# Attention and mixture of experts in one kernel: heads handled by twos, a product moved between turned rows, and the first planned expert fetched a step sooner

## The chip, the cores and the metric

The kernel runs on one core of one Trainium2 chip. The metric is the device time of one execution in microseconds; the time before is the median of three timed runs. The profile is of one further execution.

## The reference, cut to what matters

Block-sparse attention over 4 batches, 8 heads, 768 tokens, head size 64, in blocks of 32 tokens (24 blocks): the first and last block row see all keys ("dense"), every other block row sees its three neighbours, the first and last block and three drawn blocks ("sparse"). Each of the 3072 attended tokens then goes to one of 8 experts.

```python
scores = np.where(mask, q @ k.T / sqrt(64), -1e9)
x = softmax(scores) @ v                      # tokens x 512
e = argmax(x @ w_gate)
out[t] = p_e(t) * sigmoid(x @ w_output_gate)[t, e] * (relu(x[t] @ w1[e]) @ w2[e])
```

## The kernel before, in words

**Steps.** The kernel is one long program of numbered steps. A batch pair (`bp` 0, then 1) has 26 units: 4 dense ones (`Dense(bp, u)`, u = 0 to 3, each for the head pair u and u + 4 of both batches) and 22 sparse ones (`Sparse`, two for each of 11 pairs of block rows). Step n starts unit n. So steps 0 to 3 are dense, 4 to 25 sparse, 26 to 29 dense, 30 to 51 sparse. From step 27 on the experts' work is mixed in (`mixed`, L1394); a name like `p_h(0)` there is the expert program's work item 0, and its step is 31 plus its number in `program` (`FIRST` = 31).

**A unit** runs over three steps: `pS` (scores on TensorE into two PSUM banks), `dM` (row maxima on VectorE), `aE` (exponentials on ScalarE), `pT` (turning, L490: three or four 128x128 transposes of a piece on TensorE, then a copy out of PSUM by VectorE or ScalarE), one step later `pO` (the product with V), then `fin` (division by the sum, whose first instruction, L502, is the mark `normed` that POOL's indirect DMAs of that step wait for by `behind`). A dense unit has four pieces, T0 to T3; the PSUM pool `psT` has two buffers, so T2 and T3 wait for the copies of T0 and T1.

In a dense step n the order on TensorE is `pS` of unit n, `pO` of unit n - 2, T0 and T1 of unit n - 1, T2 and T3 of unit n - 1, and on VectorE `dM` of unit n, then the copies of T0 and T1 (L1417 to 1430):

```python
if isinstance(last, Dense):
    if before: before.pO()
    now.dM()
    if isinstance(now, Dense):
        last.pT(0, "dve")
        now.aE()
        last.pT(1, "act")
```

**What sets the order.** Every engine runs its instructions in the order in which the program is written. Hooks `at(step, rank, f)` put helper work behind a stage of a step: rank 0 ahead of the maxima, 2 ahead of the turning, 3 to 5 at the end. All plain DMAs are issued from SP in that order, so an SP wait holds every later one.

**K and V on chip.** `kn[bp]` holds the keys, 128 partitions x 24 blocks x 256 values (all 8 heads of a block side by side). The start loads it in two halves of 12 blocks (1.5 MB each) and V in 6 chunks of 520 KB. `gather_k`, `window_k` and `fixed` scale blocks of 256 values into the ring `kr` for the sparse units: on POOL (L412, L434), VectorE (L441, L442) and ScalarE (L432). The keys of batch pair 1 are loaded in 12 pieces at the steps of `LOAD_K`.

**The start.** `warm(n, w)` (L172) runs `NWARM[n]` matmuls on ones: 44 of 128 columns and 21 of 512 before the first scores, 11 between the two halves of them, 8 and 8 in step 1. `setup_blocks` (L322) makes the row indices for V from the drawn blocks (`raw`); it runs whole ahead of step 0 on VectorE. `setup_rest` zeroes the row table in four DMAs.

**The first planned expert (unit 0 of `EARLY`).** Its tokens are known once 8 of the 24 token tiles are routed: `route_c` ends at step 25, four `route_d` scatters write the table (`SCATTER[1]`, L804), `choose` (L757; 13 instructions on POOL with 2 and then 4 on VectorE around them) finds the expert and `load_r` reads its number into SP's registers. `load_t` (step 27, L971) reads the table rows and waits for the scatters; `load_x` (L1010, POOL, two halves) gathers the tokens; `load_w` (L987, SP) loads the weights in pieces of 512 KB; `w_h` and `w_l` (L1068 ScalarE, L1072 VectorE) split a piece in two f16 parts from step 29 on. `x_t` (L1040, TensorE, steps 29 and 30) turns the gathered tokens, `x_l` (L1047, VectorE, steps 30 and 31) makes their low part, and `p_h(0)` (L1086, step 31) is the first product with them.

## Time and profile before

| | us |
|---|---|
| timed runs, median (lowest to highest) | 549.1 (547.7 to 552.0) |
| the profiled execution's own time | 543.43 |
| its span in the profile | 541.8 |
| TensorE busy | 510.1 (94%) |
| VectorE, ScalarE, POOL busy | 357.3, 311.5, 249.0 |

The span runs from the first to the last instruction; 1.6 us of the profiled execution lie around it. In all rows times are counted from the start of the span. "PEclk" is the granted TensorE clock as a share of full speed, "DMA share" the mean busy share of 16 DMA engines.

### The profile page before, as it was taken

To read this page: it belongs to the slowest core of one execution; us is meant where nothing else is said; L and a number is where in the kernel's file an instruction comes from. 1 tells how busy PE (TensorE), PEld (TensorE's weight loads), DVE (VectorE), ACT (ScalarE), POOL (GpSimd) and SP (SyncE) were. 2 spreads that over 40 slices of the span, in tenths; PEclk is the share of its full clock that TensorE was granted. 3 is DMA by queue.
4 is the path that set the end of the run, shared out by engine and by line. 5 is a ranking of instruction groups with operands and counts; after the bars stand their busy time and mean duration, and the time that the engine had idled before them with its cause. 6 is when DMAs were issued, how large, how long until landed. Compare 5 with 4: busy or idle time off the path is not lost. (4 is left out here: it accounts for less than half of the span.)

```text
span 541.8 us, 18874 instructions
## 1 busy us (share of the span) xinstructions
PE 510.1 (94%) x7429; PEld 358.9 (66%) x7429; DVE 357.3 (66%) x732; ACT 311.5 (57%) x584; POOL 249.0 (46%) x369
## 2 busy tenths in 40 slices
PE   8999999988879999999999999999999999999993
PEld 5466676666557667776777766677666667676671
DVE  5568577585679766876876668776755754465580
ACT  1455666665666656776666555666562663554480
POOL 3466566752755855548646337553421503211120
PEclk9999999999998999999999999999999999999997
DMA  7969988889399769887767595599998999996111
GB/s 295 280 197 306 294 259 264 237 239 298 92 327 311 202 224 301 242 230 251 220 209 227 142 343 197 203 391 402 405 301 299 325 399 313 301 326 232 28 40 37
DMA packets 60062, 137.98 MB, mean 255 GB/s; under 512 B 20471, under 2 KB 27131, under 8 KB 59708
## 3 DMA queue, kind: packets, MB, share of 16 engines
q1 hardware_dynamic: 48524, 99.93, 57.0%
q0 software_dynamic: 11296, 36.49, 21.1%
q8 instruction: 60, 0.98, 0.7%
q10 hardware_dynamic: 144, 0.26, 0.2%
q14 instruction: 38, 0.31, 0.2%
HBM read 127.88 MB, written 14.81 MB: 263 GB/s over the span
## 5 line engine op out<-in xcount | busy, mean ns | idle before, releaser
L1086 PE MATMUL h<-xb,kr 128*128 128x256 f16 (+1 forms) x780 | 86.9, 261 | 1.4 <-DMA xb<-xb 1.4
L1118 PE MATMUL S<-kr,hh 128*128 128x512 f16 x348 | 85.4, 379 | 0.0
L1086 PEld LDWEIGHTS <-kr 128*128 128x128 f16 x780 | 69.5, 98 | 19.7 <-issue 2.8
L434 POOL TENSOR_TENSOR kr<-kn,eighth 128x256 f32<-128x256 f32 x110 | 68.7, 651 | 9.1 <-issue 7.1
L534 DVE TENSOR_REDUCE mx<-S 128x4 f32<-128x1024 f32 x44 | 53.7, 1219 | 28.1 <-PE S L527 16.6
L542 ACT ACTIVATE P<-S,mx 128x256 f32<-128x256 f32 x176 | 69.1, 484 | 1.1 <-DVE mx L534 1.0
L451 POOL DMA_INDIRECT vt<-in_v_dram,vidx x44 | 45.0, 1022 | 51.5 <-DVE den L504 29.0
L1118 PEld LDWEIGHTS <-hh 128*128 128x128 f16 x384 | 36.9, 98 | 30.4
L493 ACT COPY pt<-T 128x512 f32<-128x512 f32 x66 | 36.9, 592 | 31.0 <-PE T L490 28.6
L1099 ACT ACTIVATE hh<-h 128x512 f16<-128x512 f32 (+1 forms) x36 | 19.7, 548 | 55.9 <-PE h L1086 55.4
L1010 POOL DMA_INDIRECT xb<-xscr,tab x16 | 20.7, 1295 | 63.0 <-issue 23.6
L527 PE MATMUL S<-kr,qall 64*32 64x256 f32 x1408 | 49.5, 386 | 0.0
L490 PE MATMUL T<-ident,P 128*128 128x128 f32 x352 | 46.0, 274 | 0.0
L1072 DVE SCALAR_TENSOR_TENSOR kr<-e,kr 128x1024 f16<-128x1024 f32 x32 | 38.3, 1219 | 9.8 <-ACT kr L1068 9.8
L804 POOL DMA_INDIRECT table<-vals,place x24 | 26.7, 1114 | 33.1 <-DVE den L504 21.1
L490 PEld LDWEIGHTS T<-ident,P 128*128 128x128 f32 x352 | 40.1, 143 | 1.6 <-issue 1.3
L560 PE MATMUL O<-vt,pt 128*32 128x65 f32 x1408 | 32.8, 222 | 4.7 <-issue 4.1
L1105 DVE SCALAR_TENSOR_TENSOR hh<-h,hh 128x512 f16<-128x512 f32 (+1 forms) x36 | 22.5, 626 | 19.7 <-ACT hh L1099 16.6
L1072 DVE SCALAR_TENSOR_TENSOR ws<-e,ws 128x1024 f16<-128x1024 f32 x24 | 29.9, 1246 | 7.0 <-PE h L1086 4.3
L560 PEld LDWEIGHTS O<-vt,pt 128*32 128x32 f32 x1408 | 25.6, 110 | 13.0 <-issue 8.8
L1086 PEld LDWEIGHTS <-ws 128*128 128x128 f16 x324 | 29.9, 99 | 5.4 <-issue 0.4
L1068 ACT ACTIVATE kr<-e 128x1024 f16<-128x1024 f32 x32 | 33.1, 1050 | 0.0
(349 smaller groups left out, 972.5 us busy)
## 6 DMA issues: line engine op xcount, KB each, us to landing
e<-in_wcat_dram SPq DMA_DIRECT2D x80, 512.0 KB
rk<-in_wcat_dram SPq DMA_DIRECT2D x30, 512.0 KB
vc<-in_wcat_dram SPq DMA_DIRECT2D x14, 512.0 KB
vn<-in_v_dram SPq DMA_DIRECT2D x12, 520.0 KB
xscr<-x SPq DMA_DIRECT2D x48, 128.0 KB
qall<-in_q_dram SPq DMA_DIRECT2D x23, 256.0 KB
vc<-in_v_dram SPq DMA_DIRECT2D x22, 260.0 KB
ws<-in_wcat_dram SPq DMA_DIRECT2D x8, 512.0 KB
```

Of the source, the lines that this page charges most:

```text
L434: nc.gpsimd.tensor_tensor(r[:, slot], kn[bp][:, ds(rv, 1)].rearrange("p o n -> p (o n)"), eighth.to_broadcast([128, 256]), op=ALU.mult)
L451: behind(nc.gpsimd.indirect_dma_start(vt[bp, i][:, s].rearrange("p b j w -> p (b j w)"), None, v, bass.IndirectOffsetOnAxis(ap=vidx[:, bp, ...
L490: nc.tensor.transpose(pt[:, 128 * c:128 * c + 128], p[:, 128 * c:128 * c + 128], ident)
L493: mark("copy", nc.scalar.copy(t[:, 0:w], pt[:, 0:w]))
L527: nc.tensor.matmul(s[64 * h2 + 32 * qi:64 * h2 + 32 * qi + 32, b, hp], t[p, 64 * j + 32 * qi:64 * j + 32 * qi + 32], g[p, 1 - qi:3:1 + qi, ...
L534: mark("max", nc.vector.tensor_reduce(mx, self.s.rearrange("p b h n -> p (b h) n"), axis=AX.X, op=ALU.max, negate=True))
L542: nc.scalar.activation(p[:, 256 * hp:256 * hp + 256], self.s[:, b, hp], AF.Exp, bias=self.mx[:, 2 * b + hp:2 * b + hp + 1])
L560: nc.tensor.matmul(o[row:row + 32, b, hp, 0:VW], self.t[b][:, col:col + 32], av[:, qi, b, 4 * h2 + 2 * hg + hp], start=b == 0 and hp == 0, ...
L1068: nc.scalar.activation(w[:, 0], piece(n), AF.Copy, scale=SW)
L1072: nc.vector.scalar_tensor_tensor(w[:, 1], piece(n), SW, w[:, 0], op0=ALU.mult, op1=ALU.subtract)
L1086: nc.tensor.matmul(hps[n // 2][:, cols(n)], w[:, hl, 128 * c:128 * c + 128], x[:, xl, c], start=cnt == 0, stop=cnt == 11)
L1118: nc.tensor.matmul(y, a[:, k], w[:, l, 512:1024], start=n % 8 == 0 and cnt == 0, stop=n % 8 == 7 and cnt == 2)
```

## The change

K lies as 4 head pairs x 24 blocks x 64 values, V as 4 head pairs x 2 batches x 2 x 65, on the host's side and on the chip. At the start K comes in 4 loads of 768 KB, one per head pair, the first ahead of `raw`, and V in twelve of 260 KB, first head pairs 0 and 1, then, behind K's last, 2 and 3. Of the 92 warming matmuls 30 go, all of 512 columns. `setup_blocks` is cut in four parts (one ahead of step 0, one in each of steps 0 to 2), the table is zeroed in steps 2 and 3, and K of pair 1 gets other steps. In dense steps `pO` stands between the turning of T0, T1 and that of T2, T3. For the first planned expert the scatters, the end of `choose`, `load_r` and the two `load_x` come a step sooner; its first four weight pieces are all loaded at step 27 (before: 28, 28, 28, 29), the next four one step later than before.

```diff
-EARLY_X = (28, 29), (36, 36), (38, 39), (48, 49), (53, 54)
-SCATTER = {0: (18, 19, 20, 21), 1: (26, 26, 27, 27), 2: (33, 33, 34, 34), ...
+EARLY_X = (27, 28), (36, 36), (38, 39), (48, 49), (53, 54)
+SCATTER = {0: (18, 19, 20, 21), 1: (25, 25, 26, 26), 2: (33, 33, 34, 34), ...
-LOAD_K = 4, 5, 7, 9, 11, 13, 15, 17, 19, 21, 22, 23
+LOAD_K = 3, 3, 4, 5, 13, 15, 17, 19, 20, 21, 22, 23
-NWARM = 44, 21, 11, 8, 8
+NWARM = 44, 2, 8, 8
...
-        kn[bp] = big.tile([128, NB, 256], F32, tag="kn", name=f"kn{bp}", bufs=2)
+        kn[bp] = big.tile([128, 4, NB, 64], F32, tag="kn", name=f"kn{bp}", bufs=2)
...
-    def load_k(bp, c):
-        spread(nc.sync.dma_start(kn[bp][:, c], k[bp, :, c]))
-    def load_v(bp, c):
+    def load_k(bp, u, c):
+        spread(nc.sync.dma_start(
+            kn[bp][:, u, c].rearrange("p c x -> p (c x)"), k[bp, :, u, c].rearrange("p c x -> p (c x)")))
+    def load_v(bp, c, us=slice(0, 4)):
...
+    def parts(t):
+        return t.rearrange("p (u x) -> p u x", u=4)
+    def block(bp, rv):
+        return kn[bp][:, :, ds(rv, 1)].rearrange("p u o x -> p (u o) x")
...
-                nc.vector.tensor_single_scalar(r[:, slot:slot + 1], kn[bp][:, ds(rv, 1)], EXPS, op=ALU.mult)
+                nc.vector.tensor_single_scalar(parts(r[:, slot]), block(bp, rv), EXPS, op=ALU.mult)
...
-                    r[:, slot], kn[bp][:, ds(rv, 1)].rearrange("p o n -> p (o n)"), eighth.to_broadcast([128, 256]),
-                    op=ALU.mult)
+                    parts(r[:, slot]), block(bp, rv), eighth.unsqueeze(2).to_broadcast([128, 4, 64]), op=ALU.mult)
...
-                if (bp, u, half) == (0, 0, 1):
-                    warm(2, 512)
...
+    load_k(0, 0, slice(0, NB))
     setup_load()
     setup_dup()
-    load_k(0, slice(0, 12))
-    load_k(0, slice(12, 24))
+    load_k(0, 1, slice(0, NB))
+    load_k(0, 2, slice(0, NB))
...
     for c in range(6):
-        load_v(0, c)
+        load_v(0, c, slice(0, 2))
+    load_k(0, 3, slice(0, NB))
+    for c in range(6):
+        load_v(0, c, slice(2, 4))
...
-    setup_blocks()
+    blocks = setup_blocks()
+    next(blocks)
+    for n in range(3):
+        at(n, 3, next, blocks)
+    setup_rest()
...
-            at(o + (3 if bp == 0 else 2) + r, 3, fixed_v, bp, r)
+            at(o + (3 + r if bp == 0 else 3 + 2 * r), 3, fixed_v, bp, r)
...
-                        at(t0 + 5, 3, part, choose, 20, g)
+                        at(t0 + 5, 0 if g == 1 else 3, part, choose, 20, g)
                         for u in EARLY[g]:
-                            at(t0 + 6, 3, load_r, u)
+                            at(t0 + 5 if g == 1 else t0 + 6, 0 if g == 1 else 3, load_r, u)
...
-                    do(max(p - 5, (-3, 5, 5, 15)[u]), 0.6, load_w, n)
+                    do(max(p - 5, (-3, 5, 5, 15)[u]) if u else -4 if j < 4 else p - 4, 0.6, load_w, n)
...
         if isinstance(last, Dense):
-            if before:
-                before.pO()
             now.dM()
             if isinstance(now, Dense):
                 last.pT(0, "dve")
+                if before:
+                    before.pO()
...
                 last.pT(0, "act")
+                before.pO()
                 last.pT(1, "dve")
```

## Rows read from the trace of the kernel before

**Rows 1.** Busy time by stage: us, busy us of each engine, PEclk, DMA share, GB/s
```profile
0.00:6.50 6.50, 4.79 (x45) 4.89 (x46) 2.27 (x20) 1.53 (x3) 2.43 (x17) 1.00 0.54 163
6.50:20.00 13.50, 13.10 (x74) 4.78 (x73) 6.67 (x30) 2.57 (x5) 7.96 (x19) 1.00 1.00 416
60.00:100.00 40.00, 37.82 (x937) 28.09 (x939) 28.85 (x74) 27.93 (x71) 25.64 (x35) 1.00 0.86 262
140.00:145.00 5.00, 4.47 (x76) 2.92 (x78) 3.63 (x10) 2.48 (x7) 3.82 (x5) 1.00 0.03 8
160.00:170.00 10.00, 7.96 (x118) 6.17 (x126) 8.46 (x19) 4.60 (x9) 4.12 (x5) 0.83 1.04 273
180.00:500.00 320.00, 315.43 (x3866) 222.02 (x3863) 213.35 (x375) 187.75 (x312) 140.08 (x169) 1.00 0.85 280
```

**Rows 2.** Timeline of the first 16 us: start, length, engine, line, idle before
```profile
6.45 0.63 ACT L408 ACTIVATE qall<-qall 128x512 f32<-128x512 f32 x1 [3.67 <-DMA qall<-in_q_dram]
6.62 0.19 DVE L323 COPY smp<-raw 1x72 int32<-1x72 int32 x1 [3.24 <-DMA raw<-in_sampled_dram]
6.79 3.99 PEld L175 LDWEIGHTS <-ones 128*128 128x128 f16 x19 [0.28 <-issue]
7.92 0.23 DVE L336 SCALAR_TENSOR_TENSOR bad<-dd,bad 128x72 f32<-128x72 f32 x1
...
11.20 0.88 PE L593 MATMUL S<-kn,qall 64*64 64x384 f32 x8
...
14.49 0.88 PE L593 MATMUL S<-kn,qall 64*64 64x384 f32 x8
...
15.42 0.96 DVE L601 TENSOR_REDUCE mx0d<-S 128x1 f32<-128x768 f32 x1 [2.64 <-PE S L593]
```

**Rows 3.** Timeline of dense step 2
```profile
22.95 0.55 DVE L442 TENSOR_SCALAR kr<-kn 128x768 f32<-128x768 f32 x1
...
23.37 1.52 PE L593 MATMUL S<-kn,qall 64*64 64x384 f32 x16
...
25.87 0.94 DVE L601 TENSOR_REDUCE mx1d<-S 128x1 f32<-128x768 f32 x1
...
26.95 0.56 DVE L495 COPY pt0d<-T0d 128x384 f32<-128x384 f32 x1
```

**Rows 4.** Timeline of TensorE, steps 29 to 31
```profile
155.61 0.66 PE L1040 MATMUL O<-ident,e 128*128 128x128 f32 x4 [0.85 <-DMA e<-xscr,tab]
...
162.85 0.63 PE L1040 MATMUL O<-ident,e 128*128 128x128 f32 x4 [2.04 <-DMA e<-xscr,tab]
...
167.55 1.48 PE L1086 MATMUL O<-e,ws 128*128 128x256 f16 x12
```

**Rows 5.** Timeline of VectorE, steps 29 to 31
```profile
154.79 0.17 DVE L688 COPY lsum<-lp 128x16 f32<-128x16 f32 x1 [1.42 <-issue]
...
160.47 0.56 DVE L495 COPY pt2d<-T2d 128x384 f32<-128x384 f32 x1 [0.53 <-PE T2d L490]
...
165.44 0.68 DVE L1047 SCALAR_TENSOR_TENSOR e<-O,e 128x512 f16<-128x512 f32 x1
```

**Rows 6.** Timeline of POOL and SP, steps 26 to 28
```profile
134.93 1.08 POOL L804 DMA_INDIRECT table<-vals,place  x1 [7.76 <-DVE den L504]
...
144.86 0.65 SPq L971 DMA_DIRECT2D tab<-table  x1
...
147.21 1.48 SPq L987 DMA_DIRECT2D e<-in_wcat_dram  x3
...
147.83 1.00 POOL L1010 DMA_INDIRECT e<-xscr,tab  x1 [1.48 <-ACT pt2d L493]
```

**Rows 7.** Timeline of POOL, the same product on strided and contiguous operands
```profile
7.04 0.27 POOL L229 TENSOR_TENSOR dupd<-dupf 128x48 f32<-128x48 f32 x1
7.38 0.27 POOL L230 TENSOR_TENSOR dupd<-dupd 128x48 f32<-128x48 f32 x1
```

**Rows 8.** Page: costliest groups, POOL's products of key blocks
```profile
L434 POOL TENSOR_TENSOR kr<-kn,eighth 128x256 f32<-128x256 f32 x110 | 68.7, 651 | 9.1 <-issue 7.1
```

More of the change, by code (lines that the diff above doesn't have):

```diff
@@ L343, in setup_blocks @@
         nc.vector.tensor_tensor(sf, sf, t0, op=ALU.add)
+        yield
         tab = sp.tile([128, NPAIR, 2], F32, name="tab")
@@ L351, in setup_blocks @@
         for g in range(4):
+            if g == 2:
+                yield
             pp = slice(32 * g, 32 * g + 32)
@@ L360, in setup_blocks @@
         nc.vector.tensor_copy(vidx[:, 1], tab)
+        yield
     def setup_rest():
@@ L367, in setup_rest @@
         for f in range(4):
-            at(cur[0] + f, 3.3, fill, f, tz)
+            at(2 + f // 2, (3.3, 3.6)[f % 2], fill, f, tz)
     def fill(f, tz):
@@ L381, in tile_kernel @@
     kr = [ring.tile([128, 12, 256], F32, name=f"kr{i}") for i in range(RK)]
-    vc = [ring.tile([128, 2, 8, VW], F32, name=f"vc{i}") for i in range(RC)]
+    vc = [ring.tile([128, 4, 2, 2, VW], F32, name=f"vc{i}") for i in range(RC)]
     qall = ring.tile([128, RQ, 512], F32, name="qall")
@@ L388, in prep_alloc @@
     def prep_alloc(bp):
-        kn[bp] = big.tile([128, NB, 256], F32, tag="kn", name=f"kn{bp}", bufs=2)
+        kn[bp] = big.tile([128, 4, NB, 64], F32, tag="kn", name=f"kn{bp}", bufs=2)
     def prep_alloc_v(bp):
-        vn[bp] = big.tile([128, 6, 2, 8, VW], F32, tag="vn", name=f"vn{bp}", bufs=1)
-    def load_k(bp, c):
-        spread(nc.sync.dma_start(kn[bp][:, c], k[bp, :, c]))
-    def load_v(bp, c):
-        spread(nc.sync.dma_start(vn[bp][:, c].rearrange("p b j w -> p (b j w)"), v[769 * bp + 128 * c:769 * bp + 128 * c + 128]))
+        vn[bp] = big.tile([128, 6, 4, 2, 2, VW], F32, tag="vn", name=f"vn{bp}", bufs=1)
+    def load_k(bp, u, c):
+        spread(nc.sync.dma_start(
+            kn[bp][:, u, c].rearrange("p c x -> p (c x)"), k[bp, :, u, c].rearrange("p c x -> p (c x)")))
+    def load_v(bp, c, us=slice(0, 4)):
+        n = VROW // 4
+        spread(nc.sync.dma_start(
+            vn[bp][:, c, us].rearrange("p u b h w -> p (u b h w)"),
+            v[769 * bp + 128 * c:769 * bp + 128 * c + 128, n * us.start:n * us.stop]))
     qt, vt = {}, {}
@@ L529, in pS @@
                                 t[p, 64 * j + 32 * qi:64 * j + 32 * qi + 32],
-                                g[p, 1 - qi:3:1 + qi, :, 32 * j:32 * j + 32], start=True, stop=True)
+                                g[p, 1 - qi:3:1 + qi, :, n:n + 32], start=True, stop=True)
         def dM(self):
@@ L561, in pO @@
                                 o[row:row + 32, b, hp, 0:VW], self.t[b][:, col:col + 32],
-                                av[:, qi, b, 4 * h2 + 2 * hg + hp], start=b == 0 and hp == 0, stop=False)
+                                av[:, qi, 2 * hg + hp, b, h2], start=b == 0 and hp == 0, stop=False)
             for b in range(2):
@@ L568, in pO @@
                             o[64 * h2:64 * h2 + 64, b, hp, 0:VW], self.t[b][:, col:col + 64],
-                            cv[:, b, 4 * h2 + 2 * hg + hp], start=False, stop=b == 1 and hp == 1)
+                            cv[:, 2 * hg + hp, b, h2], start=False, stop=b == 1 and hp == 1)
         def fin(self):
@@ L594, in pS @@
                             self.s[b][64 * h2:64 * h2 + 64, half, 0:384], t[p, 64 * j:64 * j + 64],
-                            kn[bp][p, 12 * half:12 * half + 12, 32 * j:32 * j + 32], start=True, stop=True)
+                            kn[bp][p, u, 12 * half:12 * half + 12, 32 * h2:32 * h2 + 32], start=True, stop=True)
         def dM(self):
@@ L628, in pO @@
                             o[64 * h2:64 * h2 + 64, b, 0, 0:VW], t[:, col + 64 * h2:col + 64 * h2 + 64],
-                            vn[bp][:, c, b, 4 * h2 + u], start=b == 0 and c == 0, stop=b == 1 and c == 5)
+                            vn[bp][:, c, u, b, h2], start=b == 0 and c == 0, stop=b == 1 and c == 5)
         def fin(self):
@@ L931, in piece @@
             pool4["k"] = big.tile([128, 6, 1024], F32, tag="kn", name="rk", bufs=2)
-        v = [t.rearrange("p b j w -> p (b j w)")[:, 0:1024] for t in vc]
+        v = [t.rearrange("p u b h w -> p (u b h w)")[:, 0:1024] for t in vc]
         a, b = early_buffers(0), early_buffers(1)
@@ L1408, in tile_kernel @@
         if step == 1:
-            warm(3, 512)
+            warm(2, 512)
         enters = isinstance(now, Dense) and isinstance(last, Sparse)
```

36 lines of the change are left out of this document (19 added, 17 removed).

## The prediction

> **What bounds the kernel now.** Read first the busy times by stage [rows 1]. From 180 to 500 us TensorE is busy for 315.43 of 320 us at full clock, from 60 to 100 us for 37.82 of 40: there TensorE sets the pace, and the change takes no work from it there. The time to be won lies at the two ends of that view's middle. One is the start. DMA moves 163 GB/s over the first 6.5 us and 416 from then to 20 us [rows 1], and TensorE only warms up until 11.20 us. The timeline of the start shows why the first maxima begin no sooner than 15.42 us: scores of the first half at 11.20, of the second half at 14.49 [rows 2]. Nothing overtakes that: each later dense step hangs on the one before by the chain scores, maxima, exponentials or copies, scores. The other is 160 to 170 us: TensorE busy for 7.96 of 10 us at a granted clock of 0.83, VectorE for 8.46, the DMA engines for all of it (1.04), whereas from 140 to 145 us they stood idle (0.03) [rows 1]. There TensorE waits twice for the gathered tokens, 0.85 and 2.04 us [rows 4].
>
> **The start.** New, the first scores need q (0.26 MB) and one head pair of K (0.79 MB). By 6.5 us 163 GB/s x 6.5 us = 1.06 MB had moved [rows 1], so they land at 6.5 to 7.2. q was there at 6.45 and its scaling ended at 7.08 [rows 2]. The warming is no obstacle any more: 19 of the 21 wide matmuls began at 6.79 [rows 2] and all of these go, with the 11 between the halves. So the scores can start at 7.2; a whole block of them takes 1.52 [rows 3]: 8.7. VectorE must first do the eight index instructions on `raw`, which took 6.62 to 8.15 [rows 2], 1.53 us; `raw` now comes behind the first K load, I take 7.6, so they end at 9.1. The maxima start at 9.1 instead of 15.42: 6.3 us won.
>
> From there the chain per step is the same instructions, so the lead stays, if nothing arrives late. Landing times at 416 GB/s from 6.5 us on: K of pair 2 (2.62 MB with q) 10.3; half of V (4.2 MB) 14.2; K's last part (5.0 MB) 16.1; all of V (6.6 MB) 20. In the old timeline less 6.3 they are wanted at 17.1 (scores of step 2, 23.37 before), about 18.6 (`pO` of unit 0, behind those scores), 22 (step 3) and 28. All have 4 us of cover or more, except what reads whole blocks: `window_k` in step 1 waits for K's last part, behind the third part of the index setup on VectorE. Two copies, this part (eight instructions at the 0.19 us of the first eight, 1.5 us) and `window_k` (0.55 for its larger half [rows 3], some 0.8 in all) stand between the turning of step 1 and the maxima of step 2, where VectorE had about 2.4 us free (turning of T2 and T3 and 1.52 of scores). I take 0.4 as late, between 0 and 0.8. So the start gives 5.9. Bounds: 6.7 if `raw` comes along with K; 4.9 if K's first part is only complete when 1.9 MB have moved, at 8.5 us, and VectorE loses the 0.8.
>
> **The other orders of step 0 to 4.** `pO` behind T0 and T1: in step 2 the maxima ended at 25.87 + 0.94 = 26.81 and the first copy began at 26.95 [rows 3], 0.14 late because T0 was turned only behind `pO`. That goes, and no more, since VectorE's maxima are next. Step 3 has the same pattern; in the steps from dense to sparse (4 and 30) T2 follows `pO` without waiting for ScalarE's copy. I put 0.5 us on all of bp 0, 0.3 on steps 28 and 29; bounds 0 and 1.5 together. Eight more load instructions on SP and the earlier zeroing are hidden: DMA was at its ceiling already, SP only feeds it.
>
> **The first planned expert.** Two scatters move to step 25, behind its mark. The tokens are gathered at 147.83 and the second half a step later [rows 6], while weights issued from 147.21 fill the DMA engines; TensorE waits until 155.61 and 162.85 [rows 4]. New: the last two scatters stand where those of step 26 stood, from 134.93 on at 1.08 each [rows 6], so they are issued by 137.3; table rows wait for their landing, some 2 us (an estimate: the first rows were asked for at 144.86, a step behind), so 139.5 instead of 144.86. The four weight pieces (2.1 MB) are issued at 133 to 136, right ahead of the stretch with a DMA share of 0.03 [rows 1]; at 302 GB/s (163 / 0.54, the first stretch of [rows 1] taken to a full share) they take 7 us and are in by 144 even behind V's last chunks. The table load stands behind them on SP, so tokens are gathered at 144 and 148, in by 147 and 151, cover 7 us or more. Both waits go. What is queued behind: `choose` now makes VectorE wait at rank 0 of step 26, ahead of its two maxima, for POOL, which does two scatters and 6 small instructions behind the mark of step 25. POOL stood idle for 7.76 us ahead of 134.93, from 127.2 on [rows 6]; the scatters (2.5 with what lies between) and six instructions of the size of [rows 7] (1.6) end near 132, with 0.7 for the mark. The maxima, 0.95 each [rows 3], had to end ahead of the mark at 134.9, so they began near 132.7: no cost, but only about 0.7 us of cover; each us beyond it is a us of the chain. SP reads the expert's number in step 26 and holds q and the last V chunks for about 2 us; they are wanted a step and more later.
>
> How much of the waits comes out: 0.85 + 2.04, and the clock: a mean of 0.83 is a third of the 10 us at 1.2 GHz in place of 2.4, which costs 0.17 x 10 = 1.7 us [rows 1]; 4.6 in all. But VectorE is next. From the copy at 154.79 to the end of `x_l` at 165.44 + 0.6 [rows 5] it stands idle 0.53 at 160.47 [rows 5] and hardly elsewhere (busy 8.46 of the 10 us from 160 on [rows 1], the rest behind `x_l`); all else is work that stands ahead of `x_l` in its queue, and `p_h(0)` waits for `x_l`. So `x_l` ends 0.5 us sooner, with the 0.3 of steps 28 and 29 at 165.2, and `p_h(0)` starts there instead of at 167.55 [rows 4]: 2.35. TensorE then waits for VectorE for about 1.9 us at that place. Bounds: 0.3 and 4.9.
>
> **Strided blocks.** The 110 products on POOL, 651 ns each [rows 8], and those on the other engines read four runs of 64 in place of 256. Nearest rows: the product on strided operands (L229) took 0.27 us, the contiguous one of the same size (L230) 0.27 [rows 7]. I take nothing; if each grew, POOL idle for 14.4 of 40 us [rows 1] takes it up. Lower bound nothing too.
>
> **The sum.** 5.9 + 0.5 + 2.35 = 8.75, I take 8.7. On the profiled execution's 543.43: 534.7. The timed runs have a median 5.7 us higher; on it 549.1 - 8.7 = 540.4. From 180 us on TensorE carries the lead through unchanged, since loads are issued as it frees their buffers.
>
> **The rivals.**
> 1. *The clock still falls in step 31.* The wait for VectorE of 1.9 us is as long as the 2.04 ahead of the old fall. For it: the length. Against: it comes behind a full step without the wait of 0.85. 1.7 us come back: 542.1.
> 2. *The clock falls in the start,* where 30 warming matmuls are gone. Against: the granted clock reads 1.00 there [rows 1], with waits of about half a microsecond. Price: a score block of 1.52 and the turning, about 1 us, at half clock add 1.3 us in each of three steps, 3.9: 544.3. The Trainium skill, "TensorE: Matmul & The Clock Gate", Part 1, says that the engine is throttled unless activity releases it, which is this rival; only the step into 160 to 170 us shows such a fall here.
> 3. *The small loads don't stream.* At the 302 GB/s of the first stretch V's half would come at 16.9 and K's last part at 19.5, about 20.5 with 1 us lost between loads; `window_k` would hold VectorE until then in place of 18.3, 2.2 us. With a little on the first load too, 2.6 us of the gain go: 543.0. For it: 768 and 260 KB in place of 1.5 MB and 520 KB. Against: 520 KB pieces ran at 416 GB/s with a share of 1.00 [rows 1], so a queued load hides the one before. The Trainium skill, "DMA: Bandwidth & Descriptors", section Bandwidth, asks for 1 MiB or more in a DMA and puts some 2 us of fixed time on each; taken one by one, by that rule K's last part, eleventh in line, would come near 35 and the kernel would be slower than before, about 557. The rate of 416 in 520 KB pieces speaks against such a reading.
> 4. *All waits come out,* VectorE catching up: 4.9 in place of 2.35: 537.9.
> 5. *The tokens are late all the same,* since their table load now stands behind four weights on SP: 5.9 + 0.5: 542.7.
> 6. *Slower: POOL becomes the bound.* In the 40 us from 60 it makes about 4.5 x 5 products (937 matmuls [rows 1] at some 200 for a pair of block rows) and has 14.4 idle, so each may grow by 0.64 us; beyond that every 0.1 us on 110 products is 11 us. From a product of 0.651 + 0.64 + 0.08 = 1.37 us on, the 8.7 are lost; at 1.5 the kernel takes about 555. For it: four short runs and a broadcast over two dimensions are a form that the trace lacks. Against: [rows 7].
>
> **How the numbers follow.** Forecast 0.48; rivals 1 to 6: 0.15, 0.07, 0.10, 0.06, 0.08, 0.06. About 1%, 5.5 us, can be told from no change: 543.6 and 554.6 are the limits. Faster by more: 0.87 of the forecast, 0.8 of rival 1, 0.3 of 2, 0.6 of 3, all of 4, 0.7 of 5: 0.73. Slower by more: most of rival 6, 0.05. Within: 0.22. The range goes from 536.5 (rival 4 with the start's upper bound) to 546.5 (the start's gain lost), and leaves out rival 6 and some scatter of runs.
>
> **What would show it.** Maxima of step 0 at 9 us, every later score block of the first steps about 6 us sooner (that of step 2 near 17.4 in place of 23.37); no wait for DMA ahead of the two L1040; weights issued near 134; VectorE busy without a gap up to `x_l` and TensorE waiting ahead of `p_h(0)`; POOL's products still 0.65. Wrong if the maxima of step 0 start behind 10.5, if VectorE waits for POOL in step 26, if the granted clock falls before 30 us, or if the lead at 60 us is gone by 500.

## The result, and the profile after

| | before | after |
|---|---|---|
| timed runs, median (lowest to highest), four each | 549.64 (547.7 to 552.0) | 540.73 (538.65 to 542.85) |
| ratio, 95% interval | | 0.9858 [0.9813, 0.9904] |
| the profiled execution's own time | 543.43 | 542.85 |
| its span | 541.8 | 541.2 |

The kernel became faster by 1.4%: 7.8 us by the ratio, with an interval from 5.3 to 10.3 (the medians lie 8.9 apart). The forecast of 540.4 is met within 0.4 us. The two profiles alone would not show it: before's lay below all four timed runs of before, after's is the slowest of its four, and their spans differ by 0.6 us. What follows therefore compares places, and every place over several profiles.

The view of busy time by stage for the kernel after answers to [rows 1] (us, busy us of TensorE, its weight loads, VectorE, ScalarE, POOL, then granted clock, DMA share, GB/s):

```profile
0.00:6.50 6.50, 4.55 (x46) 4.16 (x46) 2.26 (x20) 1.91 (x3) 2.43 (x17) 1.00 0.52 168
6.50:20.00 13.50, 11.64 (x90) 5.33 (x92) 9.31 (x30) 5.49 (x12) 4.41 (x13) 1.00 1.00 392
45.00:50.00 5.00, 4.18 (x59) 3.65 (x66) 1.47 (x6) 1.05 (x5) 2.40 (x4) 0.66 0.84 256
140.00:145.00 5.00, 4.80 (x77) 3.36 (x72) 3.36 (x8) 3.02 (x7) 0.97 (x1) 1.00 0.72 197
160.00:170.00 10.00, 9.28 (x211) 7.39 (x211) 9.86 (x23) 6.15 (x14) 6.01 (x7) 1.00 0.57 175
```

The small loads fill the DMA engines at the start (share 1.00). The empty stretch before 145 us is used (0.72 for 0.03). From 160 to 170 us TensorE is busy for 9.28 us at full clock, where before it was busy for 7.96 at 0.83. New is the row from 45 us on: a granted clock of 0.66, where before had 1.00.

The start, by the timeline of the kernel after; it answers to [rows 2, 3]. Of every timeline only the lines that matter are shown:

```profile
6.76 1.52 PE L608 MATMUL S<-kn,qall 64*64 64x384 f32 x16 [0.50 <-ACT qall L418]
8.09 0.19 DVE L323 COPY smp<-raw 1x72 int32<-1x72 int32 x1 [4.72 <-DMA raw<-in_sampled_dram]
9.53 0.95 DVE L616 TENSOR_REDUCE mx0d<-S 128x1 f32<-128x768 f32 x1
...
17.48 1.52 PE L608 MATMUL S<-kn,qall 64*64 64x384 f32 x16
18.59 0.42 ACT L448 ACTIVATE kr<-kn 128x256 f32 x1 [0.53 <-DMA kn<-in_k_dram]
18.60 0.30 DVE L456 TENSOR_SCALAR kr<-kn 128x256 f32<-128x256 f32 x1 [0.71 <-issue]
18.75 1.51 POOL L425 TENSOR_TENSOR kr<-kn,eighth 128x256 f32<-128x256 f32 x2 [6.87 <-DMA kn<-in_k_dram]
18.81 0.97 DVE L457 TENSOR_SCALAR kr<-kn 128x768 f32<-128x768 f32 x1
19.70 0.95 DVE L616 TENSOR_REDUCE mx0d<-S 128x1 f32<-128x768 f32 x1
...
22.98 1.52 PE L608 MATMUL S<-kn,qall 64*64 64x384 f32 x16
23.14 0.61 DVE L360 COPY tab<-sf 32x11 f32<-32x11 f32 x1
24.24 0.66 DVE L360 COPY tab<-sf 32x11 f32<-32x11 f32 x1
25.81 0.95 DVE L616 TENSOR_REDUCE mx0d<-S 128x1 f32<-128x768 f32 x1
```

Scores at 6.76, maxima at 9.53 in place of 15.42, scores of step 2 at 17.48 in place of 23.37: 5.89 us sooner both times. Then two maxima come late. Those of step 2 stand 0.70 behind the end of their scores (17.48 + 1.52), because `window_k` waited for K's last part until 18.60 (the profile lists its wait as "issue"; ScalarE's product from the same K, at 18.59, names the DMA). Those of step 3 stand 1.31 behind (22.98 + 1.52): the fourth part of the index setup (making the row indices for V) is ahead of them, with four copies, three of which take 0.56 to 0.66 us (0.16 elsewhere).

TensorE of the kernel after around the first planned expert, steps 29 to 31, by the timeline; it answers to [rows 4]:

```profile
151.72 1.11 PE L1055 MATMUL O<-ident,e 128*128 128x128 f32 x4 [0.30 <-issue]
...
159.45 0.66 PE L1055 MATMUL O<-ident,e 128*128 128x128 f32 x4 [1.39 <-DVE e L1062]
...
163.40 1.47 PE L1101 MATMUL O<-e,ws 128*128 128x256 f16 x12 [0.72 <-DVE e L1062]
```

VectorE in the same stretch, for [rows 5]:

```profile
158.71 0.68 DVE L1062 SCALAR_TENSOR_TENSOR e<-O,e 128x512 f16<-128x512 f32 x1
162.67 0.68 DVE L1062 SCALAR_TENSOR_TENSOR e<-O,e 128x512 f16<-128x512 f32 x1
```

VectorE's part of `choose`, POOL and SP in steps 25 to 28, for [rows 6]:

```profile
129.02 0.17 DVE L801 TENSOR_REDUCE epr<-epv 128x2 f32<-128x16 f32 x1 [2.15 <-POOL epv L800]
129.63 0.96 DVE L616 TENSOR_REDUCE mx0d<-S 128x1 f32<-128x768 f32 x1
132.43 2.10 SPq L1002 DMA_DIRECT2D e<-in_wcat_dram  x4
140.22 0.65 SPq L986 DMA_DIRECT2D tab<-table  x1
144.03 1.02 POOL L1025 DMA_INDIRECT e<-xscr,tab  x1 [7.55 <-DVE dend L520]
```

No wait for DMA is left. TensorE now waits for `x_l` twice: ahead of the second token half's transposes (1.39) and ahead of `p_h(0)` (0.72). The first transposes took 1.11 for 0.66 before, as the granted clock fell during them (0.50 from 152 to 155 us). `choose` made VectorE wait 2.15 us for POOL, but the maxima of step 26 began at 129.63, when their scores (128.06 + 1.52) ended: hidden, with nothing to spare. POOL's products, from the page [rows 8], did not grow:

```profile
L450 POOL TENSOR_TENSOR kr<-kn,eighth 128x256 f32<-128x256 f32 x110 | 69.5, 657 | 7.3 <-issue 6.7
```

A lead that was won can be lost again, so the most useful table is one that no view gives directly: how long the stretches between the starts of certain steps' scores take, for every profiled execution (columns: start of step 4, then step to step; in us, from the timelines of the scores).

```
                 S4     4-7    7-8   8-10  10-25  29-33  33-35  35-36  36-51   span
before          33.65  13.05   4.58   9.45  64.37  27.14  14.48   7.50  99.08  541.8
before_again    33.78  13.37   5.35   9.16  64.62  27.62  13.25  10.73  99.80  546.5
order_only      33.09  12.62   4.94   9.44  64.90  29.26  14.54   7.33 100.24  545.5
expert_only     34.09  13.52   4.70   8.56  64.55  27.00  13.94   7.73  99.44  547.2
start_only      28.99  12.91   7.66   7.41  63.52  28.69  13.75   8.39  99.68  541.1
after           29.09  12.55   7.95   7.48  64.77  26.35  12.74  11.11 100.74  541.2
after_again     29.03  12.64   8.65   8.56  64.54  24.87  12.73  11.03  99.78  540.1
warm_back       32.02  12.90   8.55   8.15  63.45  25.08  12.82  11.07 100.37  545.9
parts_sooner    27.06  13.84   6.94   8.50  66.38  24.94  12.74  11.06 101.34  542.1
loads_spread    29.00  12.51   5.41  10.03  64.68  24.88  12.70  11.12 100.70  542.5
spread_wider    27.19  12.21   4.78   8.18  61.17  25.31  12.67   6.26  98.08  524.4
bank_free       29.05  12.22   8.32   7.41  61.53  25.02  12.67   6.26  98.42  529.0
weights_before  28.50  13.07   6.32   7.83  62.97  25.32  13.14   6.27  98.41  530.9
wider_bank      28.67  12.81   4.58   8.70  68.37  24.97  12.69   9.43 100.12  538.5
```

The experiments stood on four chips: `before_again` and the three parts on one where before took a median of 549.2 us, `after_again`, `warm_back`, `parts_sooner` and `loads_spread` on one with 549.1, `spread_wider`, `bank_free` and `weights_before` on one with 536.1, `wider_bank` on one with 547.8. Ratios are always to before on the same chip; columns 10-25 and 35-36 differ by chip and are compared on one chip only; 29-33 is compared across chips, as no chip but perhaps that of the first pair, which is not on record, has profiles with and without the whole change. Some of those runs of before were disturbed, which the ratios leave out and the medians don't; so ratios are used below.

One thing stands behind the column 29-33. In each of the six profiles over 26 us the granted clock fell between 150 and 170 us (means of 0.83 to 0.86 over 10 us, in `start_only` over both 10 us); in the eight at 24.87 to 25.32 it reads 1.00 throughout. The six are the first pair, after among them, and the four of one chip; the eight all have start and expert and stand on the other chips. So whether the change keeps the clock up there or the chip does is open. Before against `after_again` shows what the clock is worth. TensorE's idle gaps in these steps sum to 4.0 us in before and 3.3 in `after_again`, whose two waits for `x_l` are

```profile
159.39 0.66 PE L1055 MATMUL O<-ident,e 128*128 128x128 f32 x4 [1.91 <-DVE e L1062]
...
163.58 1.47 PE L1101 MATMUL O<-e,ws 128*128 128x256 f16 x12 [0.82 <-DVE e L1062]
```

So 2.89 us of waits for tokens [rows 4] became 2.73 of waits for VectorE, two waits of T2 for copies (0.32 and 0.24 in before) went with the order of `pO`, and some 1.6 of the 2.27 us between the two are the clock, which stood at 0.83 from 160 to 170 us in before [rows 1].

### The profile page after: what moved, and what is told of

Same layout as the page of the kernel before. It is cut to its first block, busy times and chain, and to the rows that moved or that the text cites. A ratio compares the mean times of both kernels' runs of the same rounds, so it can differ in the third digit from the quotient of the medians.

```text
span 541.2 us, 18824 instructions
## 1 busy us (share of the span) xinstructions
PE 506.0 (93%) x7399; PEld 357.7 (66%) x7399; DVE 358.8 (66%) x732; ACT 311.2 (58%) x584; POOL 248.9 (46%) x369
## 5 line engine op out<-in xcount | busy, mean ns | idle before, releaser
L1025 POOL DMA_INDIRECT xb<-xscr,tab x16 | 19.2, 1201 | 61.8 <-issue 24.7
L577 PE MATMUL O<-vt,pt 128*32 128x65 f32 x1408 | 34.2, 223 | 6.2 <-issue 5.6
L584 PE MATMUL O<-vc,pt 128*64 128x65 f32 x704 | 32.1, 232 | 2.5 <-issue 2.5
```

The costliest lines, as they stand in the source:

```text
L577: nc.tensor.matmul(o[row:row + 32, b, hp, 0:VW], self.t[b][:, col:col + 32], av[:, qi, 2 * hg + hp, b, h2], start=b == 0 and hp == 0, stop ...
L584: nc.tensor.matmul(o[64 * h2:64 * h2 + 64, b, hp, 0:VW], self.t[b][:, col:col + 64], cv[:, 2 * hg + hp, b, h2], start=False, stop=b == 1 a ...
```

## The experiments

**The kernels unchanged, again.** They measure what a comparison can tell. Before against itself:

> The kernel before, unchanged. Theory 1: the profiled execution of before (543.43 us, below all its timed runs) was a lucky one, because TensorE stands still at instructions for which the profile shows no wait (issue) and the sum of these differs from one execution to the next by several us; then ratio 1.00, and this profile has a span of 545 to 550 with 3 us or more of such gaps beyond the 8 of the first profile. Rival: the gaps belong to fixed places and the profile slows or speeds the kernel by itself; then the span is again 541 to 543 with the same gaps at the same lines.

1.0007 [0.9968, 1.0046]: 0.4%, some 2 us, is the width to be reckoned with. And after, on another chip:

> The changed kernel, unchanged. Theory 1: its gain is real and its profiled execution (542.85, the slowest of four) was an unlucky one: ratio 0.984 to 0.990, and the parts measured alone (0.997 for the start, 0.997 for the expert) come out too small by chance. Rival: the parts are right and the four runs were lucky: ratio 0.993 to 0.996.

0.9916 [0.9875, 0.9956], 4.6 us (2.4 to 6.9). The gain is there again, smaller; the two intervals overlap from 5.3 to 6.9 us.

**One part at a time.** The change is three edits that can stand alone. The start without the rest (the change with these undone, and with them the edits of `choose`, `load_r`, `load_w` and `fixed_v`):

```diff
-EARLY_X = (27, 28), ...
+EARLY_X = (28, 29), ...
-SCATTER = {..., 1: (25, 25, 26, 26), ...
+SCATTER = {..., 1: (26, 26, 27, 27), ...
+            if before:
+                before.pO()
             now.dM()
             if isinstance(now, Dense):
                 last.pT(0, "dve")
-                if before:
-                    before.pO()
...
                 last.pT(0, "act")
-                before.pO()
                 last.pT(1, "dve")
```

> The change without its two other parts: the layout by head pairs, the loads and the warming of the start stay, the product with V stands again ahead of the turned rows, and the first planned expert is fetched as before. Theory 1: the start carries most of the gain: 4.5 to 6 us, ratio 0.989 to 0.992; first maxima near 9.5 us, first sparse scores near 29. Rival: the lead of the start is used up by the loads behind it, which come closer together (K of pair 1, table, V rows), so that it is gone by 60 us: ratio 0.997 to 1.00.

The expert's edits alone, in the kernel before (`EARLY_X`, `SCATTER`, `choose`, `load_r`, `load_w`, `fixed_v`):

```diff
-                    do(max(p - 5, (-3, 5, 5, 15)[u]), 0.6, load_w, n)
+                    do(max(p - 5, (-3, 5, 5, 15)[u]) if u else -4 if j < 4 else p - 4, 0.6, load_w, n)
...
-EARLY_X = (28, 29), ...
+EARLY_X = (27, 28), ...
```

> The kernel before with the fetching of the first planned expert alone a step sooner. Theory 1: both waits for the tokens go, VectorE takes the place of about half: 1 to 2.5 us, ratio 0.995 to 0.998; from the scores of step 29 to those of step 33 about 25 us in place of 27.1. Rival: nothing is won since the products wait for the low part of the tokens on VectorE anyway: ratio 1.00, and 27 us.

The order of `pO` alone, in the kernel before:

```diff
-            if before:
-                before.pO()
             now.dM()
             if isinstance(now, Dense):
                 last.pT(0, "dve")
+                if before:
+                    before.pO()
...
                 last.pT(0, "act")
+                before.pO()
                 last.pT(1, "dve")
```

> The kernel before with the product with V moved between the turned rows alone. Theory 1: worth 0.1 to 0.3 us in each of five dense steps, under 1 us: ratio 0.998 to 1.00, and the first copy of steps 2 and 3 begins right at the end of the maxima (0.14 us sooner). Rival: the copies of T0 and T1 were what the dense steps wait for, and the order is worth 2 us or more.

Ratios: start 0.9968 [0.9933, 1.0004], expert 0.9973 [0.9936, 1.0011], order 1.0002 [0.9962, 1.0042]. In us 1.8, 1.5 and -0.1, each plus or minus about 2: no single part can be told from no change by its time, and their sum of 3.2 agrees with the 4.6 of `after_again`. The expectation for the start, 0.989 to 0.992, is missed: its interval leaves it out, though the lead is not gone by 60 us, as the rival had it (step 10 starts 3.1 to 4.7 us sooner than in the three other profiles of that chip). Its profile is the fastest of its twelve runs. So the parts have to be read in the table. The start brings step 4 from 33.65 or 33.78 to 28.99; the order alone to 33.09; both together (29.09) no further than the start alone. For the expert's stretch from step 29 to 33 the start alone leaves 28.69, and the parts without new expert loads range from 27.14 to 29.26. With start and expert it takes 24.87 to 25.32, save in the first profile of after (26.35, clock at 0.83 from 150 to 160 us). With the expert's edits in the kernel before it takes 27.00, where one wait of 2.91 us for `x_l` stands in the view of TensorE's waits and the granted clock falls behind it (0.83 from 160 to 170 us): the tokens are there, VectorE isn't. What the clock costs there, some 1.7 us, hides what these edits are worth alone.

**Are the warming matmuls free to go?** 19 wide ones go back ahead of the first scores:

```diff
-NWARM = 44, 2, 8, 8
+NWARM = 44, 21, 8, 8
```

> The changed kernel with 19 of the removed warming matmuls of 512 columns put back ahead of the first scores. Theory 1: TensorE's own queue then holds the first scores: they start at 11.2 in place of 6.76 us, and 4.0 to 4.5 us of the gain go. Rival: the warming paid for itself: the granted clock stays higher at some place of the first 60 us, and less than 2 us are lost.

The first scores start at 11.43 (6.76 without) and those of step 4 at 32.02 (29.03): 3.0 us of the start's lead are the warming alone. That is less than the 4.0 to 4.5 us expected. The ratio, 0.9937 [0.9902, 0.9972], leaves 3.5 us of gain where `after_again` had 4.6, a difference within the width. The clock from 6.5 to 20 us reads 1.00 with and without, in this pair.

**Why only 4.6 of 5.9 us are left at step 4.** The last three parts of the index setup each a step sooner, `window_k` of pair 0 a step later:

```diff
-    for n in range(3):
+    for n in (0, 0, 1):
         at(n, 3, next, blocks)
...
-            at(u0 - 3, 3, window_k, bp, i)
+            at(u0 - 3 if bp or i else u0 - 2, 3, window_k, bp, i)
```

> The changed kernel with VectorE's index setup a step sooner (second and third part in step 0, fourth in step 1) and the first window of K a step later (step 2). Theory 1: in the change VectorE comes 0.75 us late to the maxima of step 2 (waiting for K's last part) and 1.36 us late to those of step 3 (the fourth part runs beside POOL's products and its copies take 0.55 to 0.66 us in place of 0.16): the first sparse scores come at 27 to 27.6 in place of 29.09. Rival: the lead is lost again in the standstill of step 7, and the time of the whole is as with the change.

Step 4 starts at 27.06, 6.6 us ahead of before: the two late maxima were worth 2.0. VectorE at the same work in this kernel, by the timeline, with the setup's copies now ahead of POOL's first products:

```profile
17.05 0.16 DVE L360 COPY tab<-sf 32x11 f32<-32x11 f32 x1
18.85 0.96 DVE L616 TENSOR_REDUCE mx0d<-S 128x1 f32<-128x768 f32 x1 [1.00 <-PE S L608]
23.77 0.96 DVE L616 TENSOR_REDUCE mx0d<-S 128x1 f32<-128x768 f32 x1 [0.49 <-PE S L608]
```

The copies are back at 0.16 (the last of them stands here), and both maxima wait for their scores, as they should. Ratio 0.9867 [0.9801, 0.9933], better than `after_again` by no more than the intervals allow: against that profile on the same chip the lead is 2.5 us at step 10 (56.34 for 58.88), 0.7 at step 25 and gone at step 29 (146.90 for 146.46). Steps 10 to 25 took 66.38 for 64.54, with the clock at 0.96 from 60 to 100 us.

**Where the lead goes at step 7.** In the table the step from 7 to 8 takes 4.58 to 5.35 us in the four profiles without the new start and 6.32 to 8.65 in the seven that have it with its loads as they are. TensorE in the kernel after:

```profile
41.64 1.09 PE L544 MATMUL S<-kr,qall 64*32 64x256 f32 x32
44.28 0.43 PE L695 MATMUL O<-xT,wst 128*32 128x128 f32 x8 [1.55 <-issue]
45.82 0.70 PE L577 MATMUL O<-vt,pt 128*32 128x65 f32 x17 [0.89 <-issue]
47.96 1.70 PE L506 MATMUL T<-ident,P 128*128 128x128 f32 x8
49.59 1.09 PE L544 MATMUL S<-kr,qall 64*32 64x256 f32 x32
```

and the DMA view of the kernel after, 40 to 46 us (queue, kind: packets, MB, share of 16 engines; "instruction" is the view's own name for a kind):

```profile
q0 software_dynamic: 285, 1.06, 53.7%
q1 hardware_dynamic: 535, 0.85, 48.2%
q8 instruction: 1, 0.02, 1.3%
q14 instruction: 1, 0.01, 0.3%
```

TensorE stands still for 1.55 and 0.89 us with nothing that the profile shows to wait for, while the DMA engines are full (53.7 + 48.2%) and one instruction packet arrives in each of two queues; then the granted clock falls (0.66 from 45 to 50 us) and the turning takes 1.70 in place of 1.07. In the kernel before a gap of 0.81 stands at the same place of the program, two more follow in steps 8 and 9, and the clock stays:

```profile
48.60 0.43 PE L680 MATMUL O<-xT,wst 128*32 128x128 f32 x8 [0.81 <-issue]
51.28 1.09 PE L527 MATMUL S<-kr,qall 64*32 64x256 f32 x32
53.32 0.33 PE L560 MATMUL O<-vt,pt 128*32 128x65 f32 x9 [0.48 <-issue]
...
59.71 0.18 PE L687 MATMUL O<-fold,lt 128*128 128x16 f32 x1 [1.29 <-issue]
```

So from step 7 to step 10 the gaps sum to 2.58 us in before and 2.44 in after, all of them in step 7 there; over all profiles they sum to 1.3 to 2.6 without the new start and 2.1 to 2.9 in the seven. What after pays more on this way (15.43 us for 14.03) is the fallen clock: 0.66 over 5 us is 1.7. `weights_before`, whose clock stays at 1.00 there, takes 27.22 from step 4 to 10, as the kernels without the new start do, though it stands still for 2.34 in step 7.

Theory: loads that the change moved to steps 2 to 5 (K of pair 1, the zeroing of the table, the second half of V behind them) keep the queues full when that packet is due. First only these loads back to their old steps:

```diff
-LOAD_K = 3, 3, 4, 5, 13, 15, 17, 19, 20, 21, 22, 23
+LOAD_K = 4, 5, 7, 9, 11, 13, 15, 17, 19, 21, 22, 23
...
-            at(2 + f // 2, (3.3, 3.6)[f % 2], fill, f, tz)
+            at(3 + f, 3.3, fill, f, tz)
```

> The changed kernel with the zeroing of the table and the loads of K of pair 1 at the steps of the kernel before. Theory 1: TensorE's standstill between the scores of step 7 and 8 (7.95 us from one to the next where the kernel before takes 4.6 to 5.4; gaps of 1.55 and 0.89 us without a wait, right ahead of an instruction packet landing) comes from the DMA engines being full from 20 to 45 us, so that the next instructions arrive late; with the loads spread the step takes 4 to 5.5 us, and the lead at the scores of step 8 is 4 us or more in place of 1.7. Rival: the standstill belongs to that place of the program and stays at 7.5 us or more.

Step 7 takes 5.41, but the next two 10.03 for 7.48: step 10 starts at 56.95, as in after (57.07; 58.88 in `after_again`). Ratio 0.9932 [0.9887, 0.9977]. The standstill only moved by a step, in one gap of 2.43 us. Then, together with the sooner setup (its two edits stand above), the loads spread much wider:

```diff
+LOAD_K = 7, 8, 9, 11, 12, 13, 15, 16, 17, 19, 20, 21
...
+            at((6, 10, 14, 16)[f], 3.3, fill, f, tz)
```

> The change, with two things moved: the index setup one step earlier together with K's derived blocks of pair 0 one step later, and the twelve loads of the second half's K spread over steps 7 to 21 with the zeroing of the table at steps 6, 10, 14 and 16. Theory (the standstill of step 7 comes from DMA queues kept full by the loads that the change moved to steps 2 to 5): with these loads spread TensorE's gaps of over 0.3 us without a releaser between 0 and 60 us shrink, step 7 takes 4.0 to 5.5 us instead of 7.9, the scores of step 10 start at 55 us or sooner (57.07 in the change, 60.73 before), and the ratio to the kernel before is 0.986 or less. Rival (the standstill belongs to a moment of the instruction stream and only moves, as it did when the loads were put back to their old steps): another step of 6 to 10 is 1.5 us or more longer than in the kernel before, the scores of step 10 start within 1 us of 57, and the ratio is that of the change, 0.988 to 0.994.

Step 7 takes 4.78, step 10 starts at 52.36: the theory's numbers. That is 4.6 us sooner than in `bank_free` on the same chip (57.00), 1.9 of them won by step 4. TensorE at the place:

```profile
39.40 1.09 PE L544 MATMUL S<-kr,qall 64*32 64x256 f32 x32
41.51 0.43 PE L695 MATMUL O<-xT,wst 128*32 128x128 f32 x8 [1.02 <-issue]
44.18 1.09 PE L544 MATMUL S<-kr,qall 64*32 64x256 f32 x32
```

One gap of 1.02 is left and the clock stays. But around this gap, from 40 to 42 us, the DMA engines are at a share of 0.32 and no instruction packet arrives; nor does one from 47 to 49 us in before, around the gap of 0.81. So the place of the loads bears on how long TensorE stands still, and that full queues and a late packet are the way of it is not shown. The ratio, 0.989 [0.9856, 0.9923], is that of the change and not the 0.986 or less that was expected.

**Is VectorE the bound at the expert?** The transposes of the second token half wait for VectorE to have read the first half out of the same PSUM bank. With another buffer:

```diff
-        xp = obank[1] if u == 0 else ...
+        xp = obank[1] if a == 0 else ...
```

> The change, with the transposed second half of the first planned expert's tokens in another PSUM buffer, so that it needn't wait for VectorE to read the first half out of the same bank. Theory (VectorE is the bound there, as the prediction had it): the wait of 1.39 us ahead of the second group of transposes goes, but the one ahead of the first up-projection (0.72) grows by about as much, and the scores of step 33 start less than 0.3 us sooner relative to step 29 (26.35 us apart in the change). Rival (the shared bank is a wait of its own on TensorE's path): the two steps come 1 to 1.4 us closer together, 25.0 to 25.3.

From step 29 to 33 it takes 25.02. Against the 26.35 of the expectation's yardstick that would be the rival's gain, but the yardstick was a profile with a fallen clock: the kernels with the shared bank take 24.87 to 25.32 there, on that chip 25.31 and 25.32, so the buffer is worth 0.3 at most. TensorE in this kernel:

```profile
153.18 0.66 PE L1055 MATMUL xgp<-ident,e 128*128 128x128 f32 x4 [1.11 <-DVE pt2d L511]
...
158.42 1.36 PE L1101 MATMUL O<-e,ws 128*128 128x256 f16 x11 [1.75 <-DVE e L1062]
```

and in `spread_wider`, with the shared bank on the same chip:

```profile
150.40 0.66 PE L1055 MATMUL O<-ident,e 128*128 128x128 f32 x4 [1.90 <-DVE e L1062]
...
154.58 1.47 PE L1101 MATMUL O<-e,ws 128*128 128x256 f16 x12 [0.95 <-DVE e L1062]
```

The wait ahead of the transposes fell to 1.11 (the other buffer is one that VectorE, too, has to empty first), the one ahead of the product grew to 1.75; their sum is 2.86 for 2.85. What one wait gives back the other takes. VectorE is the bound. Ratio 0.99 [0.9867, 0.9934].

**What are the early weights worth?** The weights where they stood, tokens and rows sooner as in the change:

```diff
-                    do(max(p - 5, (-3, 5, 5, 15)[u]) if u else -4 if j < 4 else p - 4, 0.6, load_w, n)
+                    do(max(p - 5, (-3, 5, 5, 15)[u]), 0.6, load_w, n)
```

> The change, with the first planned expert's weight loads where they stood before (behind the gathers, from about 144 us on), its rows, tokens and scatters a step sooner as in the change. Theory (the tokens were the late thing and the weights' place serves them only by leaving the DMA queues free): tokens still land in time or at most 1 us late, the weights come behind them and are wanted from the first up-projection on, so TensorE waits 0.5 to 2 us for DMA there; from the scores of step 29 to those of step 33 it takes 26.5 to 28 us (26.35 in the change, 27.1 to 27.6 before). Rival (the place of the weights is worth nothing): 26.35 +- 0.2 and no DMA wait. Other rival (weights issued together with the gathers hold the tokens up as before): a DMA wait ahead of the token transposes of 0.8 us or more comes back.

Three pieces are issued at 137.23, the tokens asked for at 137.93, and nothing waits for DMA; 25.32 from step 29 to 33, as in `spread_wider` on the same chip (25.31). Steps 33 to 35 take 13.14 for 12.67, so the later weights cost 0.5 us there at most, and the ratio of 0.9894 [0.9859, 0.9929] tells no difference. So the place of the weights does nearly nothing here; what is left of the expert's edits is the rows and tokens a step sooner (no run without them stands on this chip).

**Both helpful moves together** (spread loads, sooner setup, free bank; their edits stand above), on a fourth chip:

> The change with both helpful moves together: the setup parts a step earlier and the loads of K spread wider, and the second token half's transposes in a PSUM buffer of their own. Theory (the loads of steps 2 to 5 made the standstill of step 7, whatever the chip): step 7 takes 4.0 to 5.5 us, the scores of step 10 start between 51.5 and 54 us, and the ratio to the kernel before is 0.982 to 0.990. Rival (the standstill was absent in the run before only by the chip or the execution): step 7 or a neighbour takes 6 us or more, and the scores of step 10 start at 55 us or later. For step 35: 6.3 us if its groups of matmuls came from these loads, 10 to 11 if they come from the execution or the chip.

Step 7 takes 4.58 and the way from step 4 to 10 26.1 us in all (28.0 in after): on two chips of two the standstill without a releaser in step 7 is down to one gap (1.02, 0.83), about that of before (0.81). Step 10 starts at 54.76, between the theory's numbers and the rival's. 1.5 us are lost in the start. Busy time by stage of this kernel, of the stretch from 6.5 us:

```profile
6.50:20.00 13.50, 11.96 (x78) 5.28 (x76) 9.62 (x34) 5.05 (x12) 4.83 (x14) 0.87 1.01 393
```

and its TensorE there, by the timeline:

```profile
11.62 3.37 PE L608 MATMUL S<-kn,qall 64*64 64x384 f32 x16 [1.46 <-ACT P01d L625]
18.82 1.52 PE L608 MATMUL S<-kn,qall 64*64 64x384 f32 x16
```

The clock fell in step 1 (0.87 for the stretch): the scores take 3.37 in place of 2.46, the next start at 18.82 in place of 17.34. And steps 10 to 25 take 68.37, 4 us more than in `after_again`, with the clock at 0.96 from 60 to 100 us; whether the spread loads, which now fall into them, do that or the chip is open, since `spread_wider` lost nothing there against `bank_free` on one chip (61.17 and 61.53). Ratio 0.9915 [0.9878, 0.9952]. No variant beats the change by more than the measurement can tell.

## Why the prediction was right, point by point

**The time** was right, the sum of 8.7 us probably too large. The changed kernel won 7.8 us once (5.3 to 10.3, which holds 8.7) and 4.6 the second time, and that second interval (2.4 to 6.9) leaves 8.7 out. Read from the table the steps give less as well: 4.6 to 4.8 us at step 4; from there to step 10 27.2 us on average in the four profiles without the new start and 28.6 in the seven with it and its loads as they are, so 1.4 go back; some 2.3 at the expert. That is about 5.5, inside both measured intervals. That the time was met to 0.4 us is in part chance: the same kernel run again took a median of 542.96.

**The first maxima** were put at 9.1 and came at 9.53: the index work began at 8.09, not 7.6. That the chain then carries the lead unchanged held for two steps (5.89 us at step 2).

**"What reads whole blocks"** was the right worry with the wrong size. K's last part was put at 16.1; `window_k` got it at 18.60. It was issued only at 9.94, and six pieces of V, issued from 11.80 on, were in the queues together with it (that these held it up was not tried). The maxima of step 2 were 0.70 late, within the bounds of 0 to 0.8.

**The step that failed** is "from there the chain per step is the same instructions, so the lead stays, if nothing arrives late". The chain got one more piece, the fourth part of the index setup in step 2, for which the sum has no term. Its copies stand ahead of the maxima of step 3 and took four times their length beside POOL's first products: 1.31 us. With it the start is worth 4.6, below the lower bound of 4.9 (by the terms that the prediction gives for that bound, scores at 8.5 and 0.8 lost, it comes out at 4.6: 15.42 - 10.02 - 0.8; its lower end of the range, 536.5, comes out at 537.1 in the same way, and nothing hangs on it). `parts_sooner` gives 6.6 when both late maxima go. The 0.5 us for the order of `pO` was of the right size alone (0.4 from the first scores to step 4, 22.01 us for 22.45) and nothing on top of the start, whose late maxima hide it.

**The lead's way to 180 us** was the second hole: nothing in the sum or the rivals had TensorE stand still in step 7 and the clock fall behind it. The prediction's own sign of failure, a lead at 60 us that is gone by 500, came true in the pair of profiles: 3.66 us at step 10, 5.91 at step 35, 0.64 at step 51. Of these 3.6 went in the step from 35 to 36 (11.11 for 7.50), which before run again has as well (10.73).

**The expert** was right in what waits for what: both waits for tokens gone, weights at 132.4, table at 140.2, tokens asked for at 144.0 and 148.1 (forecast 133 to 136, 139.5, 144, 148), VectorE next; 24.9 to 25.3 us in place of 27.1 and 27.6 is 1.8 to 2.7, for the 2.35 of the text, though on different chips (the first pair has 27.14 and 26.35, each with a fallen clock). The split was less right than the sum. The wait left for VectorE was put at 1.9 and is 2.7 to 2.9 in `after_again`, `spread_wider` and `bank_free`, nearly the 2.89 for tokens that it replaces; most of the gain in the table is a clock that does not fall, which the change is not shown to have done. Where TensorE waits was half foreseen: ahead of `p_h(0)` and ahead of the transposes, and `bank_free` showed that the two are one. `choose` had its 0.7 us of cover used up to the last tenth: VectorE waiting for POOL in step 26 was a sign of being wrong in the prediction's own list, it came (2.15 us), and cost nothing.

**The rivals.** POOL as the bound fell: 641 to 676 ns a product in all profiles, 657 in after. Small loads that don't stream fell: 392 GB/s in pieces of 260 and 768 KB at a share of 1.00; the Trainium skill, "DMA: Bandwidth & Descriptors", section Bandwidth, asks for 1 MiB or more in a DMA, and pieces queued one behind the other did not need it here (the 2 us of fixed time that the prediction took from that page stand there in another section, for DMAs issued from GpSimd; these are issued from SP). The clock in the start (rival 2) fell in one of nine profiles with fewer warming matmuls, `wider_bank`, and cost 1.5 us there, less than the 3.9 of the text; it is what the Trainium skill, "TensorE: Matmul & The Clock Gate", Part 1, would let one expect behind waits, and in eight of nine the trace reads 1.00. The clock at the expert (rival 1) did not fall where that rival had it, behind the wait for VectorE in step 31: it reads 1.00 from 160 to 170 us in after and `after_again`, and stayed behind a wait of 2.36 in `weights_before`; it fell behind the 2.91 of `expert_only`. The fall in after comes a step sooner, from 152 us on, ahead of that wait, behind three of 0.30 to 0.42; the rival has no such case.

## What to carry to other kernels

Count what the change puts into each step for every engine, not only what it takes out of the first one: here an uncosted piece of setup took back a fifth of what the start had won. A lead won early has to be followed step by step, and over more than one execution, because TensorE can stand still later where the profile shows no wait; here the granted clock fell behind such stops in six of seven profiles, which cost more than the stops added. And before an operand's wait is removed, name the engine that stands next; here waits for tokens became waits of nearly the same length for VectorE, and two waits for that engine were one: freeing the first only filled the second.

## What the runs showed of the hardware that was not expected

- TensorE stops with nothing to wait for ("issue"): 0.81 us in step 7 of before, 1.55 + 0.89 in after, 1.02 with loads spread wide, ahead of the same product in most profiles and a few instructions later in `parts_sooner` and `loads_spread`. In after an instruction packet arrives in the same microseconds and the DMA engines are full; around the 1.02 neither is so (a share of 0.32, no packet). What holds TensorE stays open; no run changed the packets. The Trainium skill, "Runtime: NRT & Kernel Launch", section Instruction fetch mechanics, calls the cost of a refill mostly hidden; no run here shows whether it was.
- The gap can cost more than its length, where the granted clock falls after it: of the 3.4 us that step 7 took longer in after, 1.6 are gaps and the clock's 0.66 over 5 us makes up the rest.
- Step 35 is a riddle. TensorE runs its products in groups of four or five there, with 0.39 to 0.46 us between them, while the DMA engines are nearly idle (share 0.29 from 185 to 190 us). TensorE of the kernel after, by the timeline:

```profile
186.42 0.32 PE L577 MATMUL O<-vt,pt 128*32 128x65 f32 x4 [0.44 <-issue]
...
187.90 0.32 PE L577 MATMUL O<-vt,pt 128*32 128x65 f32 x5 [0.39 <-issue]
188.68 0.36 PE L577 MATMUL O<-vt,pt 128*32 128x65 f32 x9 [0.46 <-issue]
```

  It takes 11.0 to 11.1 us in five profiles of the changed kernel and its variants, 10.7 in one of before, 7.3 to 8.4 in four others, 9.4 in `wider_bank`, and 6.26 or 6.27 in all three of the chip where before takes 536 us (there the same 32 products run as one group). The granted clock from 180 to 200 us is 0.91 in the six at 10.7 to 11.1 and 1.00 in the eight others. So it comes without the change and can be missing with it; that the change makes it likelier is not ruled out, and what it is stays open.
- Small copies on VectorE from SBUF to SBUF took 0.56 to 0.66 us beside POOL's products of 0.6, and 0.16 ahead of them; `window_k`'s larger half took 0.97 or 0.55. The Trainium skill, "SBUF — State Buffer", section SBUF: two separate sides, says that the two engines share a pair of ports which one holds for its whole instruction, and the trace agrees in that the copies took about one product's length.
